# Attention followed by a hard-swish MLP on one core: crossbar transposes issued three pairs ahead, a ring of seven value tiles, rest-token padding by copies, and gated first inputs

## The chip, the cores and the metric

The kernel runs on 1 core of one Trainium2 chip. The metric is the device time of one execution in microseconds (us), lower is better. The kernel before takes 508.9 us (median of 3 runs, 508.14 to 509.29).

The core has five instruction streams that matter here: TensorE (matmul, "PE" in the profile, with its weight loads as "PEld"), VectorE ("DVE"), ScalarE ("ACT"), GpSimd ("POOL") and SyncE ("SP"), which here only issues DMA transfers. The Trainium skill, "PSUM — Partial Sum Buffer", section "Engine vs sequencer instructions", says: "ScalarE/VectorE/GpSimdE queues are strict FIFO" (first in, first out).

## The reference, cut to what matters

```python
q, k, v: (8, 12, 448, 64)          # batch, heads, tokens, head size
q_n, k_n = rmsnorm(q, g_q), rmsnorm(k, g_k)
attn = softmax(q_n @ k_n.T / sqrt(64))
x = (attn @ v)                     # then heads side by side: (3584, 768)
h = x @ w_in                       # 768 -> 2048
g = h * clip(h + 3, 0, 6) / 6
out = g @ w_out                    # 2048 -> 768, float32
```

## The kernel before

Heads are handled two at a time. There are 6 "pairs" per batch and 48 in all, numbered P. Of the 448 tokens, 384 go through the pair's own path. The last 64 of every head (the "rest") are gathered over two batches, so that they too fill 128 partitions. While batch b's attention runs, the MLP of batches b-1 and b-2 is mixed into TensorE's work. The path of one pair, with the engine of each step:

1. SP issues the loads `qk`, `vf`.
2. GpSimd squares (`sq`), VectorE sums (`ssq`), ScalarE makes 1/rms (`rs`), GpSimd scales (`qks`), GpSimd casts the values (`va`).
3. SP issues a crossbar transpose `kq <- qks`. The first 12 pairs use TensorE instead.
4. VectorE masks the keys into `kp`, and GpSimd appends the rest queries to `kq`.
5. TensorE makes scores, ScalarE exponentials (`eT`), TensorE multiplies by the values (`x_ps`), and VectorE normalises (`xn`).
6. SP transposes `xn` into `xT`. Then comes the MLP: `h_ps`, `t_sb` (ScalarE), `gT` (VectorE), `y_ps`, `y_sb` (VectorE), store (SP).

The parts that the change and the argument touch, with cuts marked:

```python
NVA = 4                                   # ring of value tiles
va_ring = [...]                           # cut
qk_pool = pool("qk_pool", 5)
v_pool = pool("v_pool", 4)
kq_pool = pool("kq_pool", 4)

def norm_pair(P):                         # sq on GpSimd, ssq on VectorE
    qk = st["qk", P]
    sq = sq_pool.tile([128, 4 * NT * D], FP32, name="sq", tag="sq")
    square(sq[:], qk[:].rearrange("p a h x -> p (a h x)"), P < 2)
    ssq = st_pool.tile([128, 4 * NT], FP32, name="ssq", tag="ssq")
    nc.vector.tensor_reduce(out=ssq[:], in_=sq[:].rearrange(...), axis=AX_X, op=A_ADD)

def prep_v(P):                            # waits until the ring's tile is free
    va = va_ring[P % NVA]
    nc.gpsimd.tensor_copy(out=va[:, :, :, 0:D], in_=vf[:].rearrange(...))

def pad_rest(b):                          # kbd on GpSimd
    for a in range(2):
        nc.gpsimd.tensor_scalar(kbd[:, :, a * 64:(a + 1) * 64],
            st["rT", b // 2][:, 0, :, e * 64:(e + 1) * 64], gmask[:, a:a + 1], None, A_MULT)

def trans_pair(P):                        # transpose and kp in one step
    ...
    if P >= 2 * NPAIR:
        nc.sync.dma_start_transpose(out=kq[:, 0:2 * SM]..., in_=qks[:]...)
    ...
    for a in range(2):
        nc.vector.tensor_scalar_mul(kp[:, a, :, 0:128], keys, gmask[:, a:a + 1])

def att_items(P):                         # what the program says beside pair P's attention
    items = [(0.0, lambda: load_step(P + 6)), (0.0, lambda: rest_step(b, j)),
             (0.0, lambda: norm_step(P + 4)),
             (0.0, lambda: trans_step(P + 2)), (0.0, lambda: prep_step(P + 3))]
    ...

with tc.manual_schedule(engines={mybir.EngineType.SP, mybir.EngineType.Pool}):
    ...                                   # the main loop
```

Inside this block the order of SP and of GpSimd is the order of the program.

Of the kernel before, what the change touches and what calls it, by code (L numbers as in the profile page):

```python
# [9 lines left out]
FP32 = mybir.dt.float32  # L10
BF16 = mybir.dt.bfloat16
# [11 lines left out]
def kernel(  # L23
# [56 lines left out]
    nc.gpsimd.memset(eps_c[:], D * 1e-6)  # L80
    nc.scalar.preload_act_table_set("natural_log_exp_and_others")

    w_in_sb = const.tile([128, NKT, DFF], BF16, name="w_in_sb")
    w_out_sb = const.tile([128, NFT, DM], BF16, name="w_out_sb")

    NVA = 4
    va_ring = []
    for i in range(NVA):
        t = const.tile([128, 2, NT, E1], BF16, name=f"va{i}")
# [3 lines left out]
    vbd_ring = []  # L93
    for i in range(NVB):
        t = const.tile([128, NPAIR, E2], BF16, name=f"vbd{i}")
        for a in range(2):
            c = a * E1 + D
            nc.vector.tensor_copy(
                out=t[:, :, c:c + 1],
                in_=mask[:, a:a + 1].unsqueeze(1).to_broadcast([128, NPAIR, 1]),  # L100
            )
        vbd_ring.append(t)


    qk_pool = pool("qk_pool", 5)
    v_pool = pool("v_pool", 4)
    sq_pool = pool("sq_pool", 2)
    st_pool = pool("st_pool", 8)
    qks_pool = pool("qks_pool", 4)
    rst_pool = pool("rst_pool", 1)  # L110
    vr_pool = pool("vr_pool", 2)
    rT_pool = pool("rT_pool", 2)
    kq_pool = pool("kq_pool", 4)
    kp_pool = pool("kp_pool", 3)
    kbd_pool = pool("kbd_pool", 3)
    e_pool = pool("e_pool", 3)
# [36 lines left out]
    def load_v(P):  # L153
        b, j = divmod(P, NPAIR)
        vf = v_pool.tile([128, 2, NT * D], FP32, name="vf")
        nc.sync.dma_start(
            out=vf[:],
            in_=v[b, 2 * j:2 * j + 2, 0:SM, :].rearrange("h (p t) d -> p h (t d)", t=NT))
        st["vf", P] = vf

    def load_pair(P):
        load_qk(P)
        load_v(P)
# [25 lines left out]
    def prep_v(P):  # L189
        vf = st.pop(("vf", P))  # L190
        va = va_ring[P % NVA]
        nc.gpsimd.tensor_copy(  # L192
            out=va[:, :, :, 0:D], in_=vf[:].rearrange("p h (t d) -> p h t d", d=D))
        st["va", P] = va

    def prep_pair(P):
        prep_qk(P)
        prep_v(P)


    def load_rest(b, i):
        if i == 0:
            st["qkr", b] = rst_pool.tile([128, 2, H, D], FP32, name="qkr")
        for e in range(2):
            (nc.scalar if b == 0 and i == 1 else nc.sync).dma_start(
                out=st["qkr", b][e * 64:(e + 1) * 64, i],
                in_=(k, q)[i][b + e, :, SM:S, :].rearrange("h p d -> p h d"))

    def load_vrest(b):
        vr = vr_pool.tile([128, NPAIR, D], FP32, name="vr")  # L210
        vv = v[b, :, SM:S, :].rearrange("(j a) p d -> a p j d", a=2)
        for a in range(2):
            (nc.scalar if b == 0 else nc.sync).dma_start(out=vr[a * 64:(a + 1) * 64], in_=vv[a])
        st["vr", b] = vr

    def prep_vrest(b, a):
        vr = st["vr", b]
        vbd = vbd_ring[b % NVB]
        dst = vbd[:, :, a * E1:a * E1 + D]
        if b == 0:  # L220
            nc.scalar.mul(dst, vr[:], mask[:, a:a + 1])
        else:
            nc.gpsimd.tensor_scalar(dst, vr[:], mask[:, a:a + 1], None, A_MULT)
        st["vbd", b] = vbd

    def norm_rest(b, i):
# [34 lines left out]
    def pad_rest(b):  # L261
        e = b % 2
        kbd = kbd_pool.tile([128, NPAIR, 128], BF16, name="kbd")
        for a in range(2):
            nc.gpsimd.tensor_scalar(  # L265
                kbd[:, :, a * 64:(a + 1) * 64], st["rT", b // 2][:, 0, :, e * 64:(e + 1) * 64],
                gmask[:, a:a + 1], None, A_MULT)
        st["kbd", b] = kbd


    def trans_pair(P):
        qks = st.pop(("qks", P))
        kq = kq_pool.tile([128, SM + S], BF16, name="kq")
        kp = kp_pool.tile([128, 2, NT, KPW], BF16, name="kp")
        st["kq", P] = kq
        st["kp", P] = kp
        if P >= 2 * NPAIR:
            nc.sync.dma_start_transpose(
                out=kq[:, 0:2 * SM].rearrange("p (t c) -> p t c", c=128),
                in_=qks[:].rearrange("p a t h d -> p (a t h d)"))  # L280
            keys = kq[:, 0:SM].rearrange("p (t c) -> p t c", c=128)
        else:
            ps = ps_M.tile([128, 2, NT, 128], BF16, name="t_ps", tag="M")
            for i in (1, 0):
                for t in range(NT):
                    nc.tensor.transpose(  # L286
                        ps[:, i, t, :], qks[:, i, t].rearrange("p h d -> p (h d)"), identity[:])
            nc.vector.tensor_copy(
                out=kq[:, SM:2 * SM], in_=ps[:, 1].rearrange("p t c -> p (t c)"))
            keys = ps[:, 0]  # L290
        for a in range(2):
            nc.vector.tensor_scalar_mul(kp[:, a, :, 0:128], keys, gmask[:, a:a + 1])  # L292
# [187 lines left out]
    def load_step(P):  # L480
        if P < NP:
            load_pair(P)

    def norm_step(P):
        if P < NP:
            norm_pair(P)
            rstd_pair(P)

    def prep_step(P):
        if P < NP:  # L490
            prep_pair(P)
        if P in (3, 5, 7, 9):
            load_w_in((P - 3) // 2)
        if 11 <= P < 15:
            load_w_out(4 * (P - 11))
            load_w_out(4 * (P - 11) + 2)

    def trans_step(P):
        if P < NP:
            trans_pair(P)  # L500
            pad_pair(P)

    def rest_step(b, j):
        n = b + 1
        if n >= B:
            return
        if j == 1:
            load_vrest(n)
        if j == 4:
            pad_rest(n)  # L510
        if j >= 4:
            prep_vrest(n, j - 4)
        if n % 2:
            return
        if j < 2:
            norm_rest(n, j)
            rstd_rest(n, j)
        elif j < 4:
            prep_rest(n, j - 2)
            if j == 3:  # L520
                trans_rest(n)
# [7 lines left out]
    def att_items(P):  # L529
        b, j = divmod(P, NPAIR)  # L530
        n = P + 1
        items = [(0.0, lambda: load_step(P + 6)), (0.0, lambda: rest_step(b, j)),
                 (0.0, lambda: norm_step(P + 4)),
                 (0.0, lambda: trans_step(P + 2)), (0.0, lambda: prep_step(P + 3))]
        if b % 2 == 0 and j == 4 and b + 2 < B:
            items += [(0.0, lambda: load_rest(b + 2, 0)), (0.0, lambda: load_rest(b + 2, 1))]
        sc = [(0.19, lambda u=u: score(n, u)) for u in range(NU)] if n < NP else []
        vs = [(0.25, lambda t=t: av(P, t)) for t in range(NT + 1)]
        items += merge(sc, vs)
        items.insert(len(items) - 6, (0.0, flush_late))  # L540

        def done():
            late.append(lambda: xtrans(P))
            if b % 2 == 1 and j % 3 == 2:
                late.append(lambda: xtrans_rest(b, j - 2))
            if j == NPAIR - 1:
                flush_late()
        items.append((0.0, done))
        return items

    def load_w_in(c):
        n = DFF // 4
        nc.gpsimd.dma_start(
            out=w_in_sb[:, :, c * n:(c + 1) * n],
            in_=moe_w_in[:, c * n:(c + 1) * n].rearrange("(t p) n -> p t n", p=128))

    def load_w_out(ft):
        nc.gpsimd.dma_start(
            out=w_out_sb[:, ft:ft + 2, :],
            in_=moe_w_out[ft * 128:(ft + 2) * 128, :].rearrange("(f p) n -> p f n", p=128))  # L560

    with tc.manual_schedule():
        load_qk(0)
        load_rest(0, 0)
        load_rest(0, 1)
        load_v(0)
        load_vrest(0)
        load_pair(1)
        load_pair(2)
        norm_pair(0)  # L570
        norm_rest(0, 0)
        rstd_pair(0)
        norm_rest(0, 1)
        rstd_rest(0, 0)
        rstd_rest(0, 1)
        make_gmask()
        prep_qk(0)
        prep_rest(0, 0)
        prep_rest(0, 1)
        trans_pair(0)  # L580
        norm_step(1)
        trans_rest(0)
        pad_pair(0)
        load_pair(3)
        for a in range(2):
            prep_vrest(0, a)
        prep_v(0)
        prep_pair(1)
        pad_rest(0)
        for u in range(NU - 1):  # L590
            score(0, u)
        norm_step(2)
        load_pair(4)
        trans_pair(1)
        pad_pair(1)
        score(0, NU - 1)
        prep_pair(2)
        norm_step(3)
        load_pair(5)

    with tc.manual_schedule(engines={mybir.EngineType.SP, mybir.EngineType.Pool}):
        for b in range(B):
# [42 lines left out]
```

## Time and profile before

| what | before | view |
|---|---|---|
| span, mean granted TensorE clock | 510.8 us, 0.963 | cores |
| TensorE busy | 440.0 us (86%) | page, part 1 |
| TensorE busy within 105-450 us | 319.7 of 345 us | windows |
| VectorE waits, kp for the transpose | 80.4 us, 30 times | waits |
| GpSimd waits, va for a free ring tile | 82.7 + 69.2 us | waits |
| the transpose's share of the chain | 12% | chain |

The page's engine line and its chain by engine (shares of the chain that ended last):

```profile
PE 440.0 (86%) x3464; PEld 259.3 (51%) x3464; DVE 244.5 (48%) x507; ACT 298.2 (58%) x583; POOL 241.7 (47%) x313
...
PE 61%; DMA 13%; POOL 13%; issue 4%; DVE 4%; SPq 2%; ACT 1%; POOLq 0%; DVEq 0%; ACTq 0%
```

The table of waits of before. Each line names the waiting engine, its instruction and what released it, then us in total, times, and longest us:

```profile
POOL va L192 <- PE r_ps L324: 82.7, 16, 9.2
DVE kp L292 <- DMA kq<-qks: 80.4, 30, 5.7
POOL va L192 <- PE r_ps L321: 69.2, 17, 7.3
...
DVE gT L410 <- ACT t_sb L408: 48.5, 54, 2.1
DVE ssq L170 <- POOL sq L142: 48.2, 26, 6.0
```

Windows of before: start and end, length, then busy us and instructions of TensorE, its weight loads, VectorE, ScalarE and GpSimd, then the granted clock, the DMA share and GB/s:

```profile
105.00:450.00 345.00, 319.69 (x2557) 188.76 (x2556) 172.28 (x354) 218.32 (x422) 154.37 (x191) 0.97 0.52 119
...
180.00:195.00 15.00, 12.60 (x99) 7.56 (x98) 4.58 (x10) 9.00 (x18) 5.11 (x6) 0.89 0.78 153
150.00:165.00 15.00, 15.00 (x121) 8.51 (x119) 8.23 (x15) 11.23 (x24) 8.75 (x11) 1.00 0.27 67
```

How to read this. The granted clock is the share of its full speed at which TensorE was allowed to run. From 105 to 450 us the kernel needs TensorE all the time, and TensorE is idle for 25.3 us (345 less 319.69). The stretch 150-165 has no hole (no idle TensorE), full clock and 121 matmul records. The stretch 180-195 has a hole of 2.4 us, a granted clock of 0.89 and 99 records. VectorE waits 80.4 us for transposes in kp, and everything behind kp in VectorE's list (gT, y_sb, xn) waits as well.

The opening of ScalarE's timeline in before (start us, us, engine, line, operation, tiles, and in brackets the idle time before it and what ended it). ACTq is ScalarE's queue issuing a transfer. The line at 9.21 comes from a narrower window and shows the second of the two merged in the line above it:

```profile
0.77 1.40 ACTq L205 DMA_DIRECT2D qkr<-in_q_dram  x2
2.20 7.60 ACTq L213 DMA_DIRECT2D vr<-in_v_dram  x2
...
9.21 0.60 ACTq L213 DMA_DIRECT2D vr<-in_v_dram  x1
...
9.91 0.84 ACT L140 ACTIVATE sq<-qk 128x768 f32<-128x768 f32 x1 [7.90 <-DMA qk<-in_k_dram]
```

The first real work of the kernel starts at 9.91 us. The bracket puts this down to the load.

### The profile page before, as it was taken

How to read it: one execution, taken by the hardware profiler on the slowest of the kernel's cores; microseconds unless marked ns; L12 is line 12 of the kernel's file. 1: busy time of each engine (PE TensorE's matmuls, PEld its weight loads, DVE VectorE, ACT ScalarE, POOL GpSimd, SP SyncE). 2: the span in 40 equal slices, each digit the busy share in tenths (PEclk: the TensorE clock that was granted, in tenths of full speed). 3: DMA queues.
4: the chain of work that ended last, by engine and by line, in shares of the span. 5: the costliest groups of instructions: out<-in, count | busy, mean ns of one | idle time of the engine just before them, and what ended most of it. 6: DMA issues, size and time to landing. Idle time of an engine off the chain costs nothing.

```text
span 510.8 us, 9231 instructions
## 1 busy us (share of the span) xinstructions
PE 440.0 (86%) x3464; PEld 259.3 (51%) x3464; DVE 244.5 (48%) x507; ACT 298.2 (58%) x583; POOL 241.7 (47%) x313
## 2 busy tenths in 40 slices
PE   0576768789969988999889979999789999999996
PEld 0344435455535645565445645565345566654563
DVE  1466555464545544553645544464354534344421
ACT  2587777676648555766558655776557666614300
POOL 2789998865544745535264645453454310000000
PEclk9999798799989989999889989999989999999999
DMA  9639999978491665549491654628433222120012
GB/s 200 186 83 249 217 212 177 168 141 188 98 204 32 173 159 91 145 95 200 92 199 36 162 147 103 162 63 212 107 94 85 71 78 61 34 63 32 31 63 62
DMA packets 123597, 63.53 MB, mean 124 GB/s; under 512 B 74400, under 2 KB 123552, under 8 KB 123552
## 3 DMA queue, kind: packets, MB, share of 16 engines
q1 hardware_dynamic: 115744, 56.06, 47.0%
q0 software_dynamic: 5440, 6.29, 8.3%
q10 hardware_dynamic: 2368, 0.59, 0.6%
q8 instruction: 27, 0.44, 0.4%
q14 instruction: 18, 0.15, 0.1%
HBM read 45.61 MB, written 11.01 MB: 111 GB/s over the span
## 4 chain that ended last, share of the span: by engine, by line
PE 61%; DMA 13%; POOL 13%; issue 4%; DVE 4%; SPq 2%; ACT 1%; POOLq 0%; DVEq 0%; ACTq 0%
PE y_ps L422 26%; PE h_ps L403 22%; DMA kq<-qks 12%; PE s_ps L312 7%; POOL sq L142 4%; PE x_ps L321 3%; POOL qks L182 3%; POOL kbd L265 1%; PE r_ps L321 1%; DMA qk<-in_k_dram 1%; PE x_ps L324 1%; DVE gT L410 1%; POOL va L192 1%; DVE kp L292 1%; POOL qkrs L240 1%
## 5 line engine op out<-in xcount | busy, mean ns | idle before, releaser
L313 ACT ACTIVATE eT<-s_ps,zero_c 128x448 bf16<-128x448 f32 x336 | 202.9, 632 | 59.5 <-PE s_ps L312 58.2
L403 PE MATMUL h_ps<-xT,w_in_sb 128*128 128x384 bf16 (+1 forms) x768 | 189.3, 363 | 16.3 <-DVE gT L410 10.1
L422 PE MATMUL y_ps<-w_out_sb,gT 128*128 128x384 bf16 x896 | 177.3, 330 | 10.0 <-DVE gT L410 9.0
L422 PEld LDWEIGHTS <-gT 128*128 128x128 bf16 x896 | 86.1, 99 | 65.6 <-issue 13.8
L408 ACT ACTIVATE t_sb<-h_ps,half_c 128x384 f32<-128x384 f32 (+1 forms) x128 | 80.8, 631 | 59.1 <-PE h_ps L403 45.2
L403 PEld LDWEIGHTS <-w_in_sb 128*128 128x128 bf16 x768 | 73.2, 99 | 75.7 <-issue 24.5
L312 PE MATMUL s_ps<-kq,kp 128*128 128x448 bf16 x288 | 105.5, 376 | 3.0 <-DVE kp L292 2.3
L410 DVE SCALAR_TENSOR_TENSOR gT<-t_sb,h_ps 128x384 bf16<-128x384 f32 (+1 forms) x128 | 78.7, 616 | 48.8 <-ACT t_sb L408 48.5
L192 POOL CAST va<-vf 128x384 bf16<-128x384 f32 x48 | 24.1, 503 | 159.6 <-PE r_ps L324 82.7
L321 PEld LDWEIGHTS <-eT 128*128 128x128 bf16 x1152 | 65.5, 102 | 39.5 <-DVE xn L340 8.1
L182 POOL TENSOR_TENSOR qks<-qk,rs 128x384 bf16<-128x384 f32 x96 | 77.4, 826 | 10.4 <-issue 8.1
L170 DVE TENSOR_REDUCE ssq<-sq 128x12 f32<-128x768 f32 x48 | 45.6, 950 | 59.2 <-POOL sq L142 48.2
L142 POOL TENSOR_TENSOR sq<-qk 128x768 f32<-128x768 f32 x46 | 67.4, 1466 | 0.1
L292 DVE TENSOR_SCALAR kp<-kq,gmask 128x384 bf16<-128x384 bf16 x72 | 27.3, 406 | 80.6 <-DMA kq<-qks 80.4
L321 PE MATMUL x_ps<-va,eT 128*128 128x65 bf16 x864 | 54.9, 198 | 5.1 <-DVE xn L340 4.9
L428 DVE COPY y_sb<-y_ps 128x384 f32<-128x384 f32 x56 | 31.0, 554 | 46.2 <-PE y_ps L422 45.3
L134 ACT ACTIVATE rs<-ssq,eps_c 128x12 f32<-128x12 f32 x48 | 14.6, 304 | 55.0 <-DVE ssq L170 55.0
L312 PEld LDWEIGHTS <-kp 128*128 128x128 bf16 x288 | 29.1, 102 | 22.4 <-issue 2.9
L324 PE MATMUL x_ps<-vbd,eT 128*128 128x130 bf16 x144 | 32.4, 225 | 0.3
L286 PE MATMUL t_ps<-identity,qks 128*128 128x128 bf16 x72 | 7.5, 250 | 26.8 <-POOL qks L182 23.9
L340 DVE TENSOR_TENSOR xn<-x_ps,rd 128x384 bf16<-128x384 f32 x48 | 26.7, 555 | 1.2
L286 PEld LDWEIGHTS <-qks 128*128 128x128 bf16 x72 | 5.3, 111 | 31.3 <-POOL qks L182 27.6
(50 smaller groups left out, 242.4 us busy)
## 6 DMA issues: line engine op xcount, KB each, us to landing
qk<-in_k_dram SPq DMA_DIRECT2D x48, 192.0 KB, 3.0
qk<-in_q_dram SPq DMA_DIRECT2D x48, 192.0 KB, 3.2
vf<-in_v_dram SPq DMA_DIRECT2D x48, 192.0 KB, 3.4
out_dram<-y_sb SPq DMA_DIRECT2D x48, 192.0 KB, 2.1
w_in_sb<-in_moe_w_in_dram POOLq DMA_DIRECT2D x4, 768.0 KB, 9.8
w_out_sb<-in_moe_w_out_dram POOLq DMA_DIRECT2D x8, 384.0 KB, 6.1
qkr<-in_k_dram SPq DMA_DIRECT2D x8, 192.0 KB, 5.9
out_dram<-y_sb SPq DMA_DIRECT2D x16, 96.0 KB, 2.2
```

The costliest lines, as they stand in the source:

```text
L142: nc.gpsimd.tensor_tensor(out=out, in0=x, in1=x, op=A_MULT)
L170: nc.vector.tensor_reduce(out=ssq[:], in_=sq[:].rearrange("p (n d) -> p n d", d=D), axis=AX_X, op=A_ADD)
L182: nc.gpsimd.tensor_tensor(out=qks[:, i].rearrange("p t h d -> p h t d"), in0=qk[:, i].rearrange("p h (t d) -> p h t d", d=D), in1=rs4[:, i ...
L292: nc.vector.tensor_scalar_mul(kp[:, a, :, 0:128], keys, gmask[:, a:a + 1])
L312: nc.tensor.matmul(out=ps[:], lhsT=lhsT, rhs=st["kq", P][:, SM:], start=True, stop=True)
L313: nc.scalar.activation(out=st["e", P][:, u, :], in_=ps[:], func=EXP, bias=zero_c[:], scale=1.0)
L321: nc.tensor.matmul(out=dst[:, a * E1:(a + 1) * E1], lhsT=eT[:, u, c0:c0 + 128], rhs=va[:, a, t, :], start=(first and a == 0 and t == 0), s ...
L324: nc.tensor.matmul(out=dst, lhsT=eT[:, 2 * NT, c0:c0 + 128], rhs=vbd[:, j, :], start=False, stop=True, skip_group_check=True)
L403: nc.tensor.matmul(out=h_ps[:, 0:n], lhsT=w_in_sb[:, kt, f * 128:(f + 1) * 128], rhs=st["xT", G][:, kt, :], start=(kt == 0), stop=(kt == N ...
L408: nc.scalar.activation(out=t_sb[:, 0:n], in_=h_ps[:, 0:n], func=RELU, bias=half_c[:], scale=1.0 / 6.0)
L410: nc.vector.scalar_tensor_tensor(out=st["gT", G][:, f, :], in0=t_sb[:, 0:n], scalar=1.0, in1=h_ps[:, 0:n], op0=A_MIN, op1=A_MULT)
L422: nc.tensor.matmul(out=y_ps, lhsT=gT[:, f, i * 128:(i + 1) * 128], rhs=w_out_sb[:, f, nh * HALF:(nh + 1) * HALF], start=(f == 0), stop=(f ...
```

## The change

The intent is to take VectorE's waits for the transposes away by issuing them one pair earlier, with one more pair of lookahead in every step before. To make that possible the value ring grows, so that GpSimd is not held up. It also relieves GpSimd of the rest-token padding in the first 100 us, and lets the first q and k land before the other transfers. The diff, cut to its core:

```diff
+    probe = const.tile([1, 1], FP32, name="probe")
-    NVA = 4
+    NVA = 7
...
+        nc.gpsimd.memset(t[:], 0.0)                       # vbd ring zeroed once
...
-    v_pool = pool("v_pool", 4)
+    v_pool = pool("v_pool", 5)
-    kq_pool = pool("kq_pool", 4)
+    kq_pool = pool("kq_pool", 5)
...
-            (nc.scalar if b == 0 else nc.sync).dma_start(out=vr[a * 64:(a + 1) * 64], in_=vv[a])
+            nc.sync.dma_start(out=vr[a * 64:(a + 1) * 64], in_=vv[a])
...
-            nc.gpsimd.tensor_scalar(dst, vr[:], mask[:, a:a + 1], None, A_MULT)
+        nc.gpsimd.tensor_copy(out=dst, in_=vr[rows])      # vbd: half the partitions
...
-            nc.gpsimd.tensor_scalar(                      # kbd
+            (nc.scalar.mul if b else nc.vector.tensor_scalar_mul)(
...                                                        # trans_pair split: transpose | keys_pair (kp)
-        items = [(0.0, lambda: load_step(P + 6)), (0.0, lambda: rest_step(b, j)),
-                 (0.0, lambda: norm_step(P + 4)),
-                 (0.0, lambda: trans_step(P + 2)), (0.0, lambda: prep_step(P + 3))]
+        items = [(0.0, lambda: load_step(P + 7)), (0.0, lambda: rest_step(b, j)),
+                 (0.0, lambda: norm_step(P + 5)), (0.0, lambda: trans_step(P + 3)),
+                 (0.0, lambda: keys_step(P + 2)), (0.0, lambda: prep_step(P + 4))]
...
         load_rest(0, 1)
+        nc.sync.dma_start(out=probe[:], in_=st["qk", 0][0:1, 1, 1, 0:1])   # waits for q and k
         load_v(0)
+        load_pair(1)
         load_vrest(0)
-        load_pair(1)
...                                                        # prologue: one more pair of each step; pad_rest(0),
                                                           # prep_v(0), prep_pair(1) go ahead of prep_vrest
+        prep_pair(3)
+        norm_step(4)
+        load_pair(6)
```

More of the change, by code (lines that the diff above doesn't have):

```diff
@@ L218, in prep_vrest @@
         vbd = vbd_ring[b % NVB]
-        dst = vbd[:, :, a * E1:a * E1 + D]
-        if b == 0:
-            nc.scalar.mul(dst, vr[:], mask[:, a:a + 1])
-        else:
-            nc.gpsimd.tensor_scalar(dst, vr[:], mask[:, a:a + 1], None, A_MULT)
+        rows = slice(a * 64, (a + 1) * 64)
+        dst = vbd[rows, :, a * E1:a * E1 + D]
+        nc.gpsimd.tensor_copy(out=dst, in_=vr[rows])
         st["vbd", b] = vbd
@@ L264, in pad_rest, with keys_pair @@
         for a in range(2):
-            nc.gpsimd.tensor_scalar(
+            (nc.scalar.mul if b else nc.vector.tensor_scalar_mul)(
                 kbd[:, :, a * 64:(a + 1) * 64], st["rT", b // 2][:, 0, :, e * 64:(e + 1) * 64],
-                gmask[:, a:a + 1], None, A_MULT)
+                gmask[:, a:a + 1])
         st["kbd", b] = kbd
     def trans_pair(P):
-        qks = st.pop(("qks", P))
         kq = kq_pool.tile([128, SM + S], BF16, name="kq")
+        st["kq", P] = kq
+        nc.sync.dma_start_transpose(
+            out=kq[:, 0:2 * SM].rearrange("p (t c) -> p t c", c=128),
+            in_=st.pop(("qks", P))[:].rearrange("p a t h d -> p (a t h d)"))
+    def keys_pair(P):
         kp = kp_pool.tile([128, 2, NT, KPW], BF16, name="kp")
-        st["kq", P] = kq
         st["kp", P] = kp
         if P >= 2 * NPAIR:
-            nc.sync.dma_start_transpose(
-                out=kq[:, 0:2 * SM].rearrange("p (t c) -> p t c", c=128),
-                in_=qks[:].rearrange("p a t h d -> p (a t h d)"))
-            keys = kq[:, 0:SM].rearrange("p (t c) -> p t c", c=128)
-        else:
+            keys = st["kq", P][:, 0:SM].rearrange("p (t c) -> p t c", c=128)
+        else:
+            qks = st.pop(("qks", P))
+            kq = kq_pool.tile([128, SM + S], BF16, name="kq")
+            st["kq", P] = kq
             ps = ps_M.tile([128, 2, NT, 128], BF16, name="t_ps", tag="M")
@@ L491, in prep_step, with keys_step @@
             prep_pair(P)
-        if P in (3, 5, 7, 9):
-            load_w_in((P - 3) // 2)
-        if 11 <= P < 15:
-            load_w_out(4 * (P - 11))
-            load_w_out(4 * (P - 11) + 2)
+        if P in (4, 6, 8, 10):
+            load_w_in((P - 4) // 2)
+        if 12 <= P < 16:
+            load_w_out(4 * (P - 12))
+            load_w_out(4 * (P - 12) + 2)
     def trans_step(P):
+        if 2 * NPAIR <= P < NP:
+            trans_pair(P)
+    def keys_step(P):
         if P < NP:
-            trans_pair(P)
+            keys_pair(P)
             pad_pair(P)
@@ L579 @@
         prep_rest(0, 1)
-        trans_pair(0)
+        keys_pair(0)
         norm_step(1)
@@ L584 @@
         load_pair(3)
+        pad_rest(0)
+        prep_v(0)
+        prep_pair(1)
         for a in range(2):
             prep_vrest(0, a)
-        prep_v(0)
-        prep_pair(1)
-        pad_rest(0)
         for u in range(NU - 1):
@@ L593 @@
         load_pair(4)
-        trans_pair(1)
-        pad_pair(1)
+        keys_step(1)
         score(0, NU - 1)
```

## The prediction

> **What bounds the kernel now.** Engine busy times in 15 us stretches split the 510.8 us span in three. (a) 15-92 us: GpSimd is busy 12 to 15 us of every 15, TensorE 9 to 12; the chain of waits there is nearly all GpSimd (sq 1.47 us, qks 2 x 0.82, kbd 2 x 1.23, vbd 1.23). (b) 92-435 us: TensorE is busy 12.2 to 15.0 of 15; hole-free stretches (105-135, 150-180, 390-435) reach 14.9 to 15.0, so nothing else limits. The holes come from the crossbar transposes: the chain holds 12% (61 us) of "DMA kq<-qks", and the wait table has VectorE kp <- DMA kq<-qks at 80.4 us, 30 times, longest 5.7. VectorE works in order, so gT, y_sb and xn queue behind and TensorE stops (its waits on gT and xn: 24 us). (c) from 435 us: MLP alone, TensorE full; untouched.
>
> A hole costs twice: the 15 us stretch with one has a granted clock of 0.89 or less, and y_ps x4 takes 1.28 us instead of 0.65. The Trainium skill, "TensorE: Matmul & The Clock Gate" (Part 1), gives half rate until about 3.4 us of sustained work; the trace agrees.
>
> **What changes.**
> - Transposes three pairs ahead: a stage (b) pair lasts about 9.6 us (345/36); a transpose lands in 3.6 us (median; worst 8.0). One more pair of lead should cover nearly all waits. From 105 to 450 us TensorE is idle 25 us, and six stretches at 0.89 lose another 10. I expect 30 of these 35 us back, plus 5 around 90-105 (an 8.0 us transpose on the chain).
> - Seven value tiles: removes GpSimd va <- PE r_ps (152 us of waits). Alone worth nothing (GpSimd isn't critical in (b)), but qks are ready early and SP's queue is freed (v loads <- va, 35 us), so the earlier transposes can really start early.
> - kbd to ScalarE (VectorE for batch 0) takes 3 x 2.46 us from GpSimd in (a). vbd: masked 1.23 us writes become half-partition copies, estimated 0.5 us each from the 0.50 us va cast; batch 0 adds two. Net about 8.5 us, of which 8 on the chain. ScalarE gains about 7 us and has room (58% busy). Zeroing vbd falls into GpSimd's idle time before 12 us.
> - Gated first inputs: the first q/k land at 9.9 us, among eight transfers; estimated 1 to 2 us earlier.
>
> Matmul work is unchanged: about 421 us at full clock (510.8 less 70.8 idle, less 3.7% of the span lost to clock).
>
> Sum: 509 - 30 - 5 - 8 - 1.5 = about **465 us**, range **456 to 480**. Chances: faster 0.97, same 0.02, slower 0.01.
>
> **What would show each step.** VectorE kp <- DMA kq<-qks falls from 80 to under 15 us, the transpose's share of the chain to under 3%; mean granted clock rises from 0.963 to about 0.98; TensorE's busy share to 90% or more; stretches of 105-435 read 14.5 or more; GpSimd's busy time falls from 242 to about 215 us, its saturated stage ends near 82 instead of 92 us; ScalarE's first square starts at 8 to 9 us; va <- r_ps waits mostly disappear.
>
> **What would make it wrong.** SP issues in order; if it sits behind stores and xn transposes, the earlier transposes start no earlier and only 10 to 15 us come back. kbd on ScalarE waits in order for the rest transpose (5.9 us) and can hold up exponentials, three times. The q/k ring (five tiles) has one pair less slack with loads seven pairs ahead; a late GpSimd would stall SP. Stage (a) may keep its gaps (qks waiting for rs, 1.5 us each), or ScalarE may replace GpSimd.

## More of the kernel before

The order of TensorE, VectorE and ScalarE is made by a scheduler when the program is built. Every tile that is reused makes a dependency that this scheduler sees.

## The result, and the profile after

The changed kernel is slower: 528.65 us (median of 4, 526.73 to 530.37) against 509.1 us (median of 4, 508.14 to 511.88) for before in the same rounds, a ratio of 1.037 (95% interval 1.032 to 1.043). Every ratio in this document is the mean time of one kernel's fast runs over the mean of the other's fast runs of the same rounds, so it is not quite the ratio of the medians quoted. All outputs are right.

The page of after, the same two lines:

```profile
PE 445.3 (85%) x3464; PEld 259.3 (49%) x3464; DVE 248.7 (47%) x509; ACT 298.9 (57%) x595; POOL 214.9 (41%) x305
...
PE 40%; DMA 17%; POOL 15%; issue 9%; DVE 8%; SPq 7%; ACT 4%; POOLq 0%; DVEq 0%; ACTq 0%
```

The waits of after:

```profile
POOL sq L144 <- DMA qk<-in_q_dram: 117.4, 22, 13.1
DVE ssq L172 <- POOL sq L144: 86.5, 37, 5.2
...
DVE gT L414 <- ACT t_sb L412: 70.6, 80, 6.5
...
POOL va L194 <- PE r_ps L325: 7.2, 2, 5.5
DVE kp L296 <- DMA kq<-qks: 5.1, 3, 3.2
```

The window of after that answers to the first one of before:

```profile
105.00:450.00 345.00, 308.85 (x2436) 179.67 (x2434) 165.32 (x337) 211.87 (x418) 131.16 (x177) 0.97 0.50 113
```

What the change was meant to do to these lines happened. The kp wait fell from 80.4 to 5.1 us, the value-ring wait from 152 us to 8.4 (7.2, and 1.2 in a line not shown), and GpSimd's busy time from 241.7 to 214.9 us. Yet TensorE is idle 36.2 us in 105-450, where it was 25.3. Two waits on the way to the scores grew: VectorE's ssq waiting for GpSimd's square (48.2 to 86.5 us), and GpSimd's square waiting for the load of q and k. That second one does not stand in before's list at all and is 117.4 us here. (VectorE's wait for ScalarE's t_sb grew too, from 48.5 to 70.6 us.)

One such stall from the timeline of after (SP, GpSimd, VectorE and TensorE picked from one window):

```profile
177.68 0.50 SPq L151 DMA_DIRECT2D qk<-in_q_dram  x1
...
182.01 1.47 POOL L144 TENSOR_TENSOR sq<-qk 128x768 f32<-128x768 f32 x1 [3.71 <-DMA qk<-in_q_dram]
...
183.51 0.95 DVE L172 TENSOR_REDUCE ssq<-sq 128x12 f32<-128x768 f32 x1 [4.64 <-POOL sq L144]
...
184.38 0.55 DVE L414 SCALAR_TENSOR_TENSOR gT<-t_sb,h_ps 128x384 bf16<-128x384 f32 x1
...
189.01 0.95 DVE L172 TENSOR_REDUCE ssq<-sq 128x12 f32<-128x768 f32 x1 [2.98 <-POOL sq L144]
189.88 0.55 DVE L414 SCALAR_TENSOR_TENSOR gT<-t_sb,h_ps 128x384 bf16<-128x384 f32 x1
...
190.48 0.81 PE L426 MATMUL y_ps<-w_out_sb,gT 128*128 128x384 bf16 x4 [2.33 <-DVE gT L414]
```

The load of q is issued at 177.68 us. GpSimd stands ready and waits 3.71 us for it. VectorE waits 4.64 us for GpSimd's square, and the gT behind it starts without any wait of its own as soon as the ssq is out of the way. Five us later the same thing repeats and stops TensorE for 2.33 us.

Where the time went, by the start of xn of single pairs (us from the span's start):

| pair | 0 | 11 | 12 | 20 | 32 | 47 |
|---|---|---|---|---|---|---|
| before | 32.95 | 108.37 | 117.23 | 196.95 | 312.09 | 447.95 |
| after | 28.86 | 111.17 | 120.89 | 205.66 | 328.21 | 463.54 |

The first result is 4.1 us earlier, and by pair 12 the kernel is 3.7 us behind. From pair 12 to 47 it takes 342.7 us where it took 330.7, another 12 us lost. The profiled spans differ by 15.1 us.

So there were two questions. What cost 12 us in the stage where 30 were expected back? And why did the first 100 us not get faster, where 13 were expected?

### The profile page after: what moved, and what is told of

Its sections match the earlier page's. It is cut to its first block, busy times and chain, and to the rows that moved or that the text cites. A ratio compares the mean times of both kernels' runs of the same rounds, so it can differ in the third digit from the quotient of the medians.

```text
span 525.9 us, 9278 instructions
## 1 busy us (share of the span) xinstructions
PE 445.3 (85%) x3464; PEld 259.3 (49%) x3464; DVE 248.7 (47%) x509; ACT 298.9 (57%) x595; POOL 214.9 (41%) x305
## 4 chain that ended last, share of the span: by engine, by line
PE 40%; DMA 17%; POOL 15%; issue 9%; DVE 8%; SPq 7%; ACT 4%; POOLq 0%; DVEq 0%; ACTq 0%
PE y_ps L426 17%; PE h_ps L407 14%; DMA qk<-in_q_dram 9%; POOL sq L144 8%; PE s_ps L316 4%; POOL qks L184 3%; SPq L151 3%; DVE ssq L172 2%; DMA xrT<-xr 2%; PE x_ps L325 2%; DMA qkr<-in_k_dram 2%; DMA rT<-qkrs 2%; ACT eT L317 2%; SPq L382 1%; DVE gT L414 1%
## 5 line engine op out<-in xcount | busy, mean ns | idle before, releaser
L316 PE MATMUL s_ps<-kq,kp 128*128 128x448 bf16 x288 | 106.8, 382 | 19.4 <-ACT eT L317 13.3
L144 POOL TENSOR_TENSOR sq<-qk 128x768 f32<-128x768 f32 x46 | 67.4, 1466 | 118.5 <-DMA qk<-in_q_dram 117.4
L414 DVE SCALAR_TENSOR_TENSOR gT<-t_sb,h_ps 128x384 bf16<-128x384 f32 (+1 forms) x128 | 79.0, 618 | 70.7 <-ACT t_sb L412 70.6
L407 PEld LDWEIGHTS <-w_in_sb 128*128 128x128 bf16 x768 | 73.6, 100 | 70.2 <-issue 20.0
L172 DVE TENSOR_REDUCE ssq<-sq 128x12 f32<-128x768 f32 x48 | 45.7, 951 | 92.8 <-POOL sq L144 86.5
L325 PEld LDWEIGHTS <-eT 128*128 128x128 bf16 x1152 | 65.6, 101 | 40.4 <-issue 8.9
L325 PE MATMUL x_ps<-va,eT 128*128 128x65 bf16 x864 | 56.3, 198 | 2.1 <-DVE xn L344 1.9
L328 PEld LDWEIGHTS <-eT 128*128 128x128 bf16 x192 | 19.0, 100 | 17.1 <-ACT eT L317 16.7
L301 POOL COPY kq<-rT 128x64 bf16<-128x64 bf16 x48 | 11.3, 235 | 31.9 <-DMA rT<-qkrs 21.1
```

The costliest lines, as they stand in the source:

```text
L144: nc.gpsimd.tensor_tensor(out=out, in0=x, in1=x, op=A_MULT)
L172: nc.vector.tensor_reduce(out=ssq[:], in_=sq[:].rearrange("p (n d) -> p n d", d=D), axis=AX_X, op=A_ADD)
L316: nc.tensor.matmul(out=ps[:], lhsT=lhsT, rhs=st["kq", P][:, SM:], start=True, stop=True)
L325: nc.tensor.matmul(out=dst[:, a * E1:(a + 1) * E1], lhsT=eT[:, u, c0:c0 + 128], rhs=va[:, a, t, :], start=(first and a == 0 and t == 0), s ...
L328: nc.tensor.matmul(out=dst, lhsT=eT[:, 2 * NT, c0:c0 + 128], rhs=vbd[:, j, :], start=False, stop=True, skip_group_check=True)
L407: nc.tensor.matmul(out=h_ps[:, 0:n], lhsT=w_in_sb[:, kt, f * 128:(f + 1) * 128], rhs=st["xT", G][:, kt, :], start=(kt == 0), stop=(kt == N ...
```

## The experiments

One more thing can be counted: the order of each engine's instructions, in the built program without a chip, or in the trace, since VectorE works in order. Counted in the traces over pairs 12 to 39, this is how many pairs ahead of xn(P) the scheduler puts ssq and kp in VectorE's list on average, beside how many pairs ahead the program lets SP load:

| kernel | loads ahead | ssq ahead of xn | kp ahead of xn |
|---|---|---|---|
| before | 6 | 5.0 | 2.45 |
| b_ring7 | 6 | 6.2 | 2.45 |
| after | 7 | 7.5 | 3.0 |
| a_ring5 | 7 | 6.0 | 3.0 |
| a_deep8 | 8 | 7.9 | 3.0 |
| a_mandve, a_ring5_mandve, a_mandve_two, a_mandve_mix | 7 | 5.0 | 2.0 |
| b_mandve | 6 | 4.0 | 2.0 |
| b_mandve_norm5 | 6 | 5.0 | 2.0 |

In after, from pair 11 to 40, ssq stands 7 or 8 pairs ahead and the loads are issued only 7 ahead. Where a quoted expectation gives 7.1 for after or 6.0 for b_ring7, the table's figures take their place; over pairs 4 to 39 the trace of after gives 7.1. In after and in b_ring7, ssq stands on average further ahead than the loads. A label with "b_" starts from the kernel before; all others start from the changed kernel. Runs sent together shared the runs of before, and these groups are given below with before's median. All runs of the experiments were fast but one of b_ring7, which was slow (539.72 us) and is not in its ratio. Two runs of before in the third call and one in the fourth were counted as slow (512.0, 512.7 and 515.7 us) and are left out of the ratios; they are in the medians given for before.

Theory O (order): the ring of seven is what hurts. GpSimd no longer waits for a value tile, so the scheduler, as I infer it, counts on its results earlier. What the built orders show is that it puts ssq (and ScalarE's rs) further ahead in the list of an in-order engine. There ssq waits for data that SP has just asked for. Rival K: ScalarE's new kbd, which waits in order for the rest transpose. Rival L: the loads are simply too late, or the deeper lookahead itself costs. Where a quoted expectation names a theory by a letter or word of its own, read it by the numbers that it gives.

### First call: ring and kbd apart (before: 511.07 us)

**a_ring5** — the change with a ring of five.

```diff
-    NVA = 7
+    NVA = 5
```

> The changed kernel with five value tiles instead of seven, nothing else. Read from the built order: the sum-of-squares reduction (ssq) that VectorE executes in order stands 7.1 pairs ahead of the normalisation xn in the changed kernel (7 or 8), 5.0 in the kernel before, and 6.0 here. Theory H (the ring lets the scheduler put ssq so early in VectorE's order that the loads, issued seven pairs ahead by SP, land too late, and VectorE stalls in order): ssq <- POOL sq falls from 86.5 us to under 45, POOL sq <- DMA qk from 117 to under 40, time 528 -> 495 to 510. Rival K (kbd on ScalarE waiting for the rest transpose is what costs): ssq waits may fall, but the time stays above 520.

**a_kbdpool** — the change with kbd back on GpSimd, ring of seven.

```diff
-            (nc.scalar.mul if b else nc.vector.tensor_scalar_mul)(
-                kbd[...], st["rT", b // 2][...], gmask[:, a:a + 1])
+            nc.gpsimd.tensor_scalar(
+                kbd[...], st["rT", b // 2][...], gmask[:, a:a + 1], None, A_MULT)
```

> The changed kernel with kbd made on GpSimd again, seven value tiles kept. Rival K: the stalls of ScalarE behind the rest transpose go (three of about 4.6 us, each followed by a TensorE hole), time falls by 8 to 15 us. Theory H: the ssq order is nearly the same (lead 7.0), time falls by 0 to 6 us, and ssq <- POOL sq stays above 70 us.

**a_ring5_kbdpool** — both edits.

> Both edits together. If H and K are separate causes the two gains add: about 490 to 500 us. If only H is true, the same as the ring of five alone within 3 us; if only K, the same as kbd on GpSimd alone.

**b_ring7** — the kernel before with nothing but the larger ring.

```diff
-    NVA = 4
+    NVA = 7
```

> The kernel before with seven value tiles, nothing else. The built order moves ssq from 5.0 to 6.0 pairs ahead of xn (loads there are issued six ahead). Theory H: no gain or slower, 508 to 522 us, ssq <- POOL sq above the 48 us of before, va <- r_ps waits (152 us) gone. If the ring only freed GpSimd and SP, as the prediction said: 495 to 508 us.

Measured:

| run | median us (range) | ratio to before (95%) |
|---|---|---|
| a_ring5 | 491.54 (490.89 to 493.98) | 0.962 (0.957 to 0.968) |
| a_kbdpool | 529.92 (529.01 to 532.31) | 1.038 (1.031 to 1.045) |
| a_ring5_kbdpool | 487.02 (486.38 to 490.19) | 0.954 (0.948 to 0.960) |
| b_ring7 | 534.80 (531.20 to 539.72) | 1.044 (1.036 to 1.052) |

The ring alone makes the kernel before 4.4% slower, more than I had expected (508 to 522 us). Taking two tiles out of the ring makes the changed kernel 37 us faster. Rival K explains none of the loss: with the ring of seven, moving kbd back changes nothing (529.92 against 528.65), while with the ring of five it is worth 4.5 us (491.54 to 487.02). A small cost was hidden behind a large one. (The expectation of a_kbdpool speaks of three stalls of 4.6 us; the trace of after has two, 6.0 us in all.) The waits of b_ring7 show the same two lines as after:

```profile
POOL sq L142 <- DMA qk<-in_q_dram: 80.2, 16, 12.0
...
DVE ssq L170 <- POOL sq L142: 68.3, 33, 6.1
```

And of a_ring5:

```profile
POOL va L194 <- PE r_ps L328: 78.9, 16, 7.5
...
DVE kp L296 <- DMA kq<-qks: 39.7, 19, 4.1
DVE ssq L172 <- POOL sq L144: 33.8, 27, 3.4
```

With five tiles GpSimd waits 78.9 us for the ring again, and the kernel is faster for it. This shows that the ring is the cause. It doesn't yet show that it acts through the order.

### Second call: the order itself, the loads, the ramp (before: 510.28 us)

**a_mandve** — ring of seven, and VectorE too in program order in the main loop. The instructions are the same; only the order changes (VectorE's, and through it what the scheduler makes of the others).

```diff
-    with tc.manual_schedule(engines={mybir.EngineType.SP, mybir.EngineType.Pool}):
+    with tc.manual_schedule(engines={mybir.EngineType.SP, mybir.EngineType.Pool, mybir.EngineType.DVE}):
```

> The changed kernel with its seven value tiles kept; only the order of VectorE's instructions in the main loop is fixed to the order in which the program issues them, instead of the scheduler's. In the built order ssq then stands 5.0 pairs ahead of xn instead of 7.5 (pairs 20 on), loads seven ahead. Theory H (the place of ssq in VectorE's order against the loads, not the ring itself, costs): ssq <- POOL sq falls below 40 us and the time to 485 to 505 although the ring is seven. If the ring costs in another way (SP, GpSimd or DMA contention when GpSimd runs free): above 518.

**a_deep8** — the scheduler's order kept, loads one pair earlier instead. The tiles for it had to be found: kp's row is cut from 144 to 136 columns. (Loads nine pairs ahead did not fit in memory and were never run.)

```diff
-    qk_pool = pool("qk_pool", 5)
-    v_pool = pool("v_pool", 5)
+    qk_pool = pool("qk_pool", 6)
+    v_pool = pool("v_pool", 6)
-    KPW = 144
+    KPW = 136
-        items = [(0.0, lambda: load_step(P + 7)), ...
+        items = [(0.0, lambda: load_step(P + 8)), ...
         load_pair(6)
+        load_pair(7)
```

> The changed kernel with loads issued eight pairs ahead instead of seven, six q/k and six value load tiles (kp rows padded to 136 instead of 144 to make room). Simple rival L (loads are just one pair too late): POOL sq <- DMA qk and ssq <- POOL sq fall by more than half, time 495 to 510. Theory H: the scheduler moves ssq ahead as far as the loads allow (built order: 7.9 pairs instead of 7.5, so loads lead by 0.1 pair), so it helps little: 515 to 530.

**ramp** — ring of five. Normalisation and preparation keep the shallow lookahead until pair 8, then go one deeper.

```diff
-                 (0.0, lambda: norm_step(P + 5)), ... (0.0, lambda: prep_step(P + 4))]
+                 (0.0, lambda: norm_ramp(P)), ... (0.0, lambda: prep_ramp(P))]
+    RAMP = 8
+    def norm_ramp(P):
+        if P <= RAMP: norm_step(P + 4)
+        if P >= RAMP: norm_step(P + 5)
+    # prep_ramp the same with P + 3 and P + 4; prologue without prep_pair(3), norm_step(4)
```

> The ring of five, with the lookahead of GpSimd's preparation kept at three pairs until pair 8 and only then raised to four (the transposes through DMA begin at pair 12). Theory F (why the first 100 us gained nothing from GpSimd's lighter work): the deeper lookahead makes GpSimd prepare a fourth pair before TensorE gets the third, which costs about 6 us once, and adds waits for rs. F expects xn of pair 11 at 102 to 106 us instead of 110, and 483 to 488 us instead of 491.5. If the fill costs nothing: 490 to 494.

**ramp_mix** — ramp, and kbd on GpSimd from batch 2 on, when GpSimd is no longer saturated.

```diff
         for a in range(2):
+            if b >= 2:
+                nc.gpsimd.tensor_scalar(kbd[...], st["rT", b // 2][...], gmask[:, a:a + 1], None, A_MULT)
+                continue
             (nc.scalar.mul if b else nc.vector.tensor_scalar_mul)(
```

> The same ramp and ring of five, and kbd off GpSimd only for the first two batches (VectorE, ScalarE), on GpSimd from batch 2 on. Expected if F and K' (kbd on ScalarE waits in order for the rest transpose, three times) hold and add: 476 to 483 us, the fastest so far; ScalarE's kbd waits gone.

Measured:

| run | median us (range) | ratio to before (95%) |
|---|---|---|
| a_mandve | 476.45 (476.35 to 476.81) | 0.934 (0.931 to 0.936) |
| a_deep8 | 506.04 (504.16 to 509.13) | 0.992 (0.988 to 0.996) |
| ramp | 488.43 (487.08 to 488.94) | 0.956 (0.954 to 0.959) |
| ramp_mix | 481.87 (478.97 to 484.06) | 0.944 (0.939 to 0.949) |

The order alone is worth 52 us on the changed kernel, ring of seven and all, and more than I had expected (485 to 505 us). Its waits:

```profile
DVE ssq L172 <- POOL sq L144: 19.6, 10, 4.8
...
ACT kbd L265 <- DMA rT<-qkrs: 13.1, 3, 7.3
```

The ssq wait fell from 86.5 to 19.6 us. Now kbd's wait of 7.3 us at its longest can be seen, which leads to a run below. a_deep8 gained 22.6 us by earlier loads, more than I had given it (515 to 530 us), though the scheduler moved ssq ahead there too (7.5 to 7.9 pairs). GpSimd's square waits 15.9 us for loads there, where it waited 117.4, and yet VectorE still waits in ssq:

```profile
DVE ssq L172 <- POOL sq L144: 59.4, 29, 8.8
```

So the lateness of the loads is a real part of the mechanism, because ssq far ahead hurts through data that is not there yet. But it is less than half of what the order gives. ramp gave 3.1 us over a_ring5 and ramp_mix another 6.6.

### Third call: is it the ring, the transposes, or the whole change? (before: 507.47 us)

**b_mandve** — the kernel before, with VectorE in program order and nothing else.

```diff
-    with tc.manual_schedule(engines={mybir.EngineType.SP, mybir.EngineType.Pool}):
+    with tc.manual_schedule(engines={mybir.EngineType.SP, mybir.EngineType.Pool, mybir.EngineType.DVE}):
```

> Control: the kernel before with nothing changed but VectorE's order in the main loop, fixed to program order (ssq 4.0 pairs ahead of xn instead of 5.0, kp 2.0 instead of 2.5). If the fixed order alone gave the 34 us that the changed kernel gains with it, this run is at 470 to 480 us as well. If the change itself gives most of it: 495 to 515 us, with kp <- DMA kq<-qks still above 60 us, since the transposes here start in the same pair in which kp reads them.

**a_ring5_mandve** — a_mandve with a ring of five.

> Changed kernel, VectorE order fixed, ring of five. Built orders of VectorE and ScalarE's first hundred instructions are those of the run with seven. Theory H says that the ring only acts through the order, so it is within 1.5% of 476.5 us (470 to 484), with va <- r_ps waits back on GpSimd but off the critical path. If seven tiles are needed for the gain: above 488.

**a_mandve_two** — a_mandve with the transposes at two pairs ahead again, all the rest of the change kept.

```diff
-                 ... (0.0, lambda: trans_step(P + 3)),
+                 ... (0.0, lambda: trans_step(P + 2)),
```

> Changed kernel, VectorE order fixed, ring of seven, but the crossbar transposes issued two pairs ahead again (in the pair whose kp reads them). If the early transposes are what gives the gain, kp <- DMA kq<-qks comes back above 60 us and the time goes to 495 to 510; if GpSimd running free is enough for them to be early: within 5 us of 476.5.

**a_mandve_mix** — a_mandve with kbd on GpSimd from batch 2 on (the edit of ramp_mix).

> Changed kernel, VectorE order fixed, seven tiles, transposes three ahead, kbd off GpSimd only for batches 0 and 1. With the order fixed ScalarE still waits 13.1 us three times for the rest transpose (kbd)[...]. Theory K' expects 460 to 470 us, the fastest; if kbd's place is worth nothing: 474 to 478.

Measured:

| run | median us (range) | ratio to before (95%) |
|---|---|---|
| b_mandve | 476.65 (473.92 to 477.41) | 0.939 (0.933 to 0.946) |
| a_ring5_mandve | 478.00 (477.71 to 479.21) | 0.944 (0.939 to 0.949) |
| a_mandve_two | 485.58 (484.33 to 490.50) | 0.957 (0.951 to 0.963) |
| a_mandve_mix | 469.07 (468.58 to 469.75) | 0.926 (0.921 to 0.930) |

Four things follow.

At a fixed VectorE order the ring is worth little: 476.45 us with seven and 478.00 with five. These are from two calls; the ratios (0.934 and 0.944) differ by 1%, about 5 us, in favour of seven. So the 37 us that seven tiles cost in the first call came through the order. Theory O stands.

b_mandve was a surprise. I had expected 495 to 515 us with more than 60 us of kp waits, since its transposes are as late as ever. It reaches 476.65 us, as fast as the whole change at the same order (476.45). Its waits:

```profile
DVE kp L292 <- DMA kq<-qks: 32.0, 14, 5.4
DVE ssq L170 <- POOL sq L142: 26.1, 11, 6.0
```

So 48.4 of the 80.4 us of kp waits in the kernel before went away with the order, the program's place of the transposes unchanged. The count points at kp standing too early in VectorE's list, on average 2.45 pairs ahead where the program says 2; no run moved kp alone.

a_mandve_two says what the early transposes are worth within the changed kernel once the order is right: 485.58 against 476.45 us, about 9 us (by the ratios, 0.957 against 0.934, 12 us). I had given that run 495 to 510 us, and its kp waits 60 us; they are 31.0 (read in the slowest of its five runs, 490.50 us):

```profile
DVE kp L296 <- DMA kq<-qks: 31.0, 13, 6.5
```

a_mandve_mix beats both kernels, by 7.4% against before; against b_mandve, what the change adds at its best is 7.6 us. Its window and page line, where 105-420 is the stage in which TensorE is the limit:

```profile
PE 424.8 (91%) x3446; PEld 255.9 (55%) x3464; DVE 249.0 (53%) x509; ACT 300.0 (64%) x583; POOL 229.7 (49%) x317
...
105.00:420.00 315.00, 313.91 (x2560) 189.09 (x2573) 174.81 (x352) 220.06 (x416) 140.28 (x184) 1.00 0.58 128
```

TensorE is busy 313.91 of 315 us at full clock there. From pair 12 to 47 it takes 294.7 us (before 330.7, after 342.7).

### Fourth call: what is still open (before: 509.61 us)

Three points were open. In b_mandve two places had moved at once (ssq from 5.0 to 4.0 and kp from 2.46 to 2.0), the gate of the first inputs had not been tried, and neither had the ramp with the order fixed.

**b_mandve_norm5** — b_mandve with ssq back at five pairs ahead.

```diff
-                 (0.0, lambda: norm_step(P + 4)),
+                 (0.0, lambda: norm_step(P + 5)),
...                                                # prologue
+        norm_step(4)
```

> The kernel before with VectorE's order fixed, and the sum of squares made one pair earlier (five ahead, as in the order that the scheduler chose for the kernel before), kp unchanged at 2.0. If the early kp (waiting for late transposes) is what held the kernel before, the time stays within 2% of 476.65 us. If the early ssq did, 490 us or more, with ssq <- POOL sq above 45 us (26 in b_mandve).

**a_mandve_mix_nogate** — a_mandve_mix without the probe.

```diff
-        nc.sync.dma_start(out=probe[:], in_=st["qk", 0][0:1, 1, 1, 0:1])
```

> The fastest version without the probe transfer that gates the later loads. The first square on ScalarE should start 3 to 4.5 us later (5.4 us with the gate, 9.9 without, in the two traces of the comparison). If that head start survives to the end: 472 to 474 us instead of 469. If it is swallowed by GpSimd's stage: 468.5 to 470.5.

**a_mandve_mix_ramp** — a_mandve_mix with the ramp edit.

> The fastest version with the lookahead raised from three to four pairs only at pair 8. Theory F (the fourth pair must be prepared before TensorE gets the third): the first xn comes back from 36.7 to about 31 us and the end is 3 to 6 us earlier, 463 to 466 us. If ScalarE or GpSimd is the limit of the first 100 us whatever the order: 468 to 471.

Measured:

| run | median us (range) | ratio to before (95%) |
|---|---|---|
| b_mandve_norm5 | 477.10 (476.21 to 481.28) | 0.938 (0.934 to 0.942) |
| a_mandve_mix_nogate | 468.82 (467.38 to 469.36) | 0.919 (0.916 to 0.923) |
| a_mandve_mix_ramp | 469.73 (468.63 to 472.48) | 0.923 (0.919 to 0.927) |

b_mandve_norm5 equals b_mandve, so ssq at 5.0 with loads at 6 costs nothing, and of the two places counted that leaves kp's as what held the kernel before. But program order fixes the places of gT, y_sb and the rest of VectorE's list as well, and those were not tried one by one, so this stays an argument.

The gate did nothing. ScalarE's first square in after, and then in a_mandve_mix_nogate:

```profile
5.35 0.84 ACT L142 ACTIVATE sq<-qk 128x768 f32<-128x768 f32 x1 [3.33 <-DMA qk<-in_q_dram]
```

```profile
5.77 0.84 ACT L142 ACTIVATE sq<-qk 128x768 f32<-128x768 f32 x1 [3.76 <-DMA qk<-in_q_dram]
```

With the gate a_mandve_mix starts it at 5.74, so removing the probe changes nothing, where I had expected 3 to 4.5 us. The 4.6 us between before (9.91) and after (5.35) therefore belong to something else that the change does in that place. The loads did not land earlier: the first q load landed 4.1 us after its issue at 1.25 us in before, and 4.0 us after 1.27 in after. But the two vr loads left ScalarE's queue. In before the second of them was issued from 9.21 to 9.81 us and the square started at 9.91. In b_mandve, which keeps these loads, the same issue starts at 8.47 and the square at 9.19; in b_ring7, at 8.28 and 8.99. I read this from the timelines; no run moved the vr loads alone.

The ramp, expected to give 3 to 6 us here (463 to 466), gave nothing: 469.73. The reason is in the timeline of VectorE around 90 us, in a_mandve_mix and then in a_mandve_mix_ramp:

```profile
89.36 0.35 DVE L401 COPY xT<-xrT 128x384 bf16<-128x384 bf16 x1 [5.92 <-DMA xrT<-xr]
```

```profile
89.89 0.35 DVE L401 COPY xT<-xrT 128x384 bf16<-128x384 bf16 x1 [7.46 <-DMA xrT<-xr]
```

These two versions meet here. xn of pair 0 starts at 36.66 us in a_mandve_mix and at 30.88 in the ramp version. At pair 9 they stand at 89.85 and 90.38. VectorE waits 5.92 us in the one and 7.46 in the other for the crossbar transpose of the rest outputs, and whatever was gained before is swallowed. SP issues this transpose at 83.15 us, behind the rest transpose (77.85) and a pair's transpose (80.12). An earlier or later place for it was not tried and stays open.

## Why the prediction was wrong, point by point

**The step that failed.** The prediction says of the seven value tiles: "Alone worth nothing (GpSimd isn't critical in (b)), but qks are ready early and SP's queue is freed". The runs show that the ring alone costs 4.4% (b_ring7) and that the ring of seven instead of five costs the changed kernel 37 us. GpSimd was not critical, that is right. But its wait for a free tile had kept the scheduler from placing VectorE's work further ahead. With that wait gone, ssq moved from 5.0 to 7.5 pairs ahead in after, and with the ring alone to 6.2 in b_ring7, beyond the loads in both (7 and 6). Then VectorE waits for GpSimd, GpSimd for the load, the load for SP, and SP for results of VectorE. One turn of this circle in after, just before the stall shown above:

```profile
174.70 0.95 DVE L172 TENSOR_REDUCE ssq<-sq 128x12 f32<-128x768 f32 x1 [2.51 <-POOL sq L144]
...
176.22 0.55 DVE L432 COPY y_sb<-y_ps 128x384 f32<-128x384 f32 x1
...
176.79 0.36 SPq L445 DMA_DIRECT2D out_dram<-y_sb  x1
177.19 0.43 SPq L151 DMA_DIRECT2D qk<-in_k_dram  x1
```

The late ssq delays y_sb, SP stores y_sb, and only then issues the load for which GpSimd waits until 182.01 us. The waits of SP in after, summed (line 445 stores y_sb, line 382 transposes xn; the VectorE instruction named is the one that came last before SP went on):

```profile
SPq L445 <- DVE y_sb L432: 68.8, 23, 7.4
SPq L382 <- DVE gT L414: 50.9, 11, 7.0
```

The first of these is no longer than in before (70.2 us), the second is (29.3 us in before). The order could have been read before the run: comparing the place of ssq in the two built programs takes a minute. I compared other places and not this one. One limit remains: the experiments moved the whole of VectorE's order. That it is ssq's place that costs is argued from the waits, the counts and a_deep8; no run moved ssq alone back, and ScalarE's rs moved together with it.

**"One more pair of lead should cover nearly all waits ... I expect 30 of these 35 us back."** The waits were covered (80.4 to 5.1 us), and the gain was there to be had: pairs 12 to 47 take 36 us less in a_mandve_mix. But the cause was only partly lateness. Program order on the old kernel recovers about 31 us (0.939 of 509) with the transposes where they were. Within the changed kernel the early transposes are worth 9 to 12 us once the order is right. As given, under the scheduler's order, the change paid for the covered waits with larger ones.

**"About 8.5 us [of GpSimd], of which 8 on the chain".** GpSimd's busy time fell to 214.9 us as predicted (about 215), but the chain did not get shorter. xn of pair 11 starts at 108.37 us in before, 111.17 in after, and 101.90 in a_mandve_mix. GpSimd stays at 14 to 15 us busy of 15 until 90 us, not 82. Part of this is the fill of the deeper lookahead: the ramp gave 3.1 us with the scheduler's order. In a_mandve_mix a VectorE wait of 5.92 us near 90 us absorbs what comes before it; in after the same wait is 2.6 us at its longest, so what took the rest there stays open.

**"Gated first inputs ... estimated 1 to 2 us earlier", square at 8 to 9 us.** It came at 5.35 us, earlier than forecast, for another reason: the probe is worth nothing. The forecast had read the 9.9 us as the landing of q and k; they landed at about 5.35 us, and the square stood in ScalarE's list behind a DMA issue that started only at 9.21 us.

**kbd on ScalarE "waits in order for the rest transpose (5.9 us) and can hold up exponentials".** This listed risk is real and of that kind: 4.5 us with the ring of five, 7.4 us at the fixed order (476.45 to 469.07; the ratios differ by 0.8%, which is 4 us, so take it as 4 to 7). Under the ring of seven it was hidden. No other risk struck as listed. SP sitting behind stores and transposes comes nearest, but what it made late were the loads, not the transposes.

**The clock.** The prediction counts 10 us for six stretches at 0.89, and cites the Trainium skill, "TensorE: Matmul & The Clock Gate", Part 1, for half rate. The traces agree that a hole can cost more than its length, but not that every hole does. In before, the 2.40 us hole that ends at 185.64 us is followed by a clock of 0.50 from 186.40 to 189.80. In after, the stretch 180-195 holds the 2.33 us stall shown above and 3.4 us of idle TensorE in all, at a clock of 1.00. The mean clock fell from 0.963 to 0.947, but from 105 to 450 us it is 0.97 in both kernels; most of the fall lies in the first 105 us (0.92 to 0.85). In a_mandve_mix, with nearly no holes from 105 to 420 us, it is 1.00 there.

The sum of 465 us was therefore close to what nearly the same work takes in another order (469 us for a_mandve_mix). It was not what this program took in the order that the scheduler gave it. That the sum comes so close is partly luck: by b_mandve, about 31 of the 40 us come from an order that the prediction did not consider.

## What to carry to other kernels

When a scheduler orders an in-order engine, a larger buffer on an idle engine need not be free: here it let work move ahead in another engine's list. So compare the built order of every in-order engine, and for each early instruction ask whether its data is even requested by then. A wait table names what ended a wait; before making the awaited thing earlier, ask whether the waiting instruction simply stands too early, and try fixing the order first, since here one line on the old kernel was worth as much as the whole change at the same order. Undo parts one by one: a cost of 4 us (kbd on ScalarE) and a gain of 9 us (early transposes) could be measured only when the larger loss above them was gone.

## What the Trainium skill lacked or had wrong

- No page says that the order a scheduler gives an in-order engine shifts with the depth of buffers elsewhere. "PSUM — Partial Sum Buffer", section "Engine vs sequencer instructions", has the strict FIFO that makes it matter. Here a ring from four to seven tiles moved ssq from 5.0 to 6.2 pairs ahead and cost 4.4%.
- "DMA: Bandwidth & Descriptors", section "DMA Transpose (X-bar)", gives constraints but no time from issue to landing, and no page gives one for SBUF to SBUF transposes of these sizes on trn2. Here the medians before are 3.6 us for 128 x 768 bf16 (up to 8.0 on the chain), 5.9 us for 128 x 1536, and 2.3 to 2.4 us for 128 x 384.
- The same page, in its sections on issuing engines, does not say that a transfer issued by ScalarE may start late and hold up the computing behind it. Here an issue of 0.60 us started 6.3 us after the one before it had ended, and the first square came at 9.91 us, though its data had landed at about 5.35.
- "TensorE: Matmul & The Clock Gate", Part 1, puts the half rate after an idle window of about 3.4 us. Here less was enough in one place: a hole of 2.40 us, in 3.41 us with 1.01 us of TensorE work, was followed by half rate (0.50) for 3.4 us. A stretch with 1.76 us of idle time (195-210 us in before) stayed at 1.00.
